# The last 64 keys of two heads as one block-diagonal product, and their flip moved behind the products with v

## The chip, the core and the metric

The kernel runs on one core of one Trainium2 chip. The metric is the device time of one execution in microseconds (us). A core has TensorE (matrix products, PE in the profile; its weight loads stand as PEld), VectorE (DVE), ScalarE (ACT), GpSimd (POOL) and SyncE (SP), which issues most transfers. Each engine works through its own list of instructions in order and waits for others by semaphores.

## The reference, cut to what matters

```python
# q, k, v: (8 batches, 8 heads, 576, 64), f32
scores = q @ k.T / sqrt(64)
scores = where(scores >= max(scores) - tau, scores, -1e9)
attn = exp(scores - max(scores)); attn /= attn.sum() + 1e-9
x = (attn @ v)                       # to (4608, 512)
g = x @ w_gate
out = (g * sigmoid(g) * (x @ w_val)) @ w_out
```

So it is an attention whose scores below a threshold are dropped, and behind it a gated feed-forward block with 512 x 1536 weights.

## The kernel before, in words

Two heads are worked together, as halves of the 128 partitions; four such pairs make a batch. The first batch is treated apart from the other seven, by code that is written out by hand (lines 411 to 755) and whose order of instructions is the order in which Python runs it. From line 758 on, the other batches are placed by a planner (`Plan`), which the change does not touch.

In the first batch a pair's 576 queries are cut into tiles of 128 (t = 0 to 3) and a last one of 64 (t = 4). The list `segs` holds first the "early" tiles t = 0, 1 of all four pairs, eight in all, and then t = 2, 3, 4 of all four pairs, twelve in all. Between the latter TensorE also makes the first products of the feed-forward block (L543). While the first batch runs, the weights are fetched (L277, L280) and taken into another form in pieces: ScalarE reads each piece twice (L296, L297), GpSimd clamps it (L289), VectorE shifts and merges it (L316, L322), GpSimd adds (L324).

A tile goes through these steps:

- `scores` (L417): products of q and k for both heads (L428, for t = 4 L434) into two `sc` tiles; VectorE takes the largest score of each row (L445); ScalarE makes the threshold and the exponential (L448, L449); VectorE drops what lies below the threshold and sums the row (L452), then takes the inverse of the sum, `ri` (L454, L455). For t below `TA` = 2 ScalarE builds per head a diagonal matrix of `ri` (L468), the `unit`; for later tiles the rows are scaled at once (L460 on GpSimd, L462 on ScalarE) and the unit is the identity.
- `flip_steps` (L479): TensorE turns the 128 x 576 values round, by a product with the unit. Per head, four blocks of 128 keys go into a bank `tp` (L496 for the early tiles, L494 later), and the last 64 keys into a bank `end` that both heads share: for the early tiles one 128*64 product per head (L499), behind that head's four blocks; for t = 2, 3 one transposition for both heads (L501); for t = 4 L505. ScalarE copies `tp` (L502) and `end` (L509) out.
- `attend_tile` (L513): the products with v. For the four blocks of 128 keys each head has a 128*64 product into its half of the bank `xa` (L526). The last 64 keys of both heads lie on the two halves of the partitions, and each head has a 64*64 product with its half of `vr2` (L529). ScalarE copies `xa` out (L531).

The loop from L691 runs these for three tiles in turn: it issues the scores of tile n, then the units of tile n - 1 (`next(last)`, L701: L468), then attends tile n - 2 (L702), then flips tile n - 1 (L703 to L709), and so ScalarE's list has L468, L531, L448, L449, L502, L509, L296, L297 in a step. Four banks of PSUM (`bank`, `give_back`, L227) go round among `xa`, `end`, `tp` and the feed-forward products. At the first tile of the second part (n = NP, x = 0) a second `attend_tile` follows in the same step (L711).

`load_v` (L394) fetches v for a pair: the first 512 keys with keys on the partitions (L407), and the last 64 keys of the first head on partitions 0 to 63, of the second head on 64 to 127 (L408), all into the tile `vall`. SyncE issues both.

Of the kernel before, what the change touches and what calls it, by code (L numbers as in the profile page):

```python
# [10 lines left out]
F32 = mybir.dt.float32  # L11
# [101 lines left out]
def kernel(  # L113
# [11 lines left out]
    nc = tc.nc  # L125
    P = 128
    B, H, S, D = q.shape
    NP = H // 2
# [6 lines left out]
    KT = S // P  # L135
    KM = KT * P
    NK = NJ // 2
    SM = 512
    NT = SM // P
# [13 lines left out]
    const = ctx.enter_context(tc.tile_pool(name="const", bufs=1))  # L153
# [22 lines left out]
    WS = NF2 * DM2  # L176
    vall = const.tile([P, 2 * NJ * D], F32, name="vall")
    PB = 24
    pall = const.tile([P, PB * SH], F32, name="pall")
    NQ = 7  # L180
    QW = NF2 // 2 * P
# [45 lines left out]
    def bank(name):  # L227
        n = turns.popleft()
        ps = ps_f.tile([P, 512], F32, name=name, tag=f"bank{n}")
        taken[id(ps)] = n, ps  # L230
        return ps

    def give_back(ps):
        turns.append(taken.pop(id(ps))[0])
# [159 lines left out]
    def load_v(seg):  # L394
        b, hp_ = divmod(seg["i"], NP)
        src = v[b, 2 * hp_:2 * hp_ + 2]
        if seg["halved"]:
            vr = vall[:, 0:NJ * D].rearrange("p (h j d) -> p h j d", h=2, d=D)
            for a in range(2):
                for c in range(2):  # L400
                    nc.sync.dma_start(out=vr[(2 * a + c) * G:(2 * a + c + 1) * G].rearrange("r h j d -> r h (j d)"),
                                      in_=src.rearrange("h (r c j) d -> c r h (j d)", c=2, j=NK)[c])
        else:
            own = vall[:, hp_ * S:(hp_ + 1) * S]
            vr = own[:, 0:2 * KT * D].rearrange("p (h t d) -> p h t d", h=2, d=D), own[:, 2 * KT * D:]
            for h in range(2):
                nc.sync.dma_start(out=vr[0][:, h], in_=src[h, 0:KM].rearrange("(t p) d -> p t d", p=P))  # L407
                nc.sync.dma_start(out=vr[1][h * D:(h + 1) * D], in_=src[h, KM:S])  # L408
        seg["v"] = vr

    heads = [slice(h * D, (h + 1) * D) for h in range(2)]

    def turned(t):
        return TA <= t < NT
# [57 lines left out]
    unflipped, unattended = deque(), deque()  # L472
    xts = {}

    def flip():
        for _ in flip_steps():
            pass

    def flip_steps():  # L479
        if not unflipped:  # L480
            return
        seg, t, both, ps = unflipped.popleft()
        n = P if t < NT else D
        pT = pTbufs[0][:, 0:2 * KT * n].rearrange("p (h t q) -> p h t q", h=2, t=KT)
        pT2 = pTbufs[0][:, 2 * KT * n:(2 * KT + 1) * n]
        pTbufs.rotate(1)
        end = bank("end")
        for h, (p, unit) in enumerate(ps):
            tp = bank("tp")
            for kt in range(KT):  # L490
                at_ = kt * P + (D if turned(t) and h == 1 else 0)
                ks, to = slice(at_, at_ + P), slice(kt * P, (kt + 1) * P)
                if unit is ident:
                    nc.tensor.transpose(tp[:, to], p[:, ks], unit)  # L494
                else:
                    nc.tensor.matmul(tp[:, to], p[:, ks], unit, start=True, stop=True)  # L496
            if t < NT:
                if not turned(t):
                    nc.tensor.matmul(end[h * D:(h + 1) * D, 0:P], p[:, KM:S], unit, start=True, stop=True)  # L499
                elif h == 1:  # L500
                    nc.tensor.transpose(end[:, 0:P], both, unit)  # L501
                nc.scalar.copy(pT[:, h], tp.rearrange("p (t q) -> p t q", q=P))  # L502
            else:
                for hs in heads:
                    nc.tensor.matmul(end[hs, 0:D], p[hs, KM:S], unit[hs, hs], start=True, stop=True)  # L505
                nc.scalar.copy(pT, tp.rearrange("p (t h q) -> p h t q", h=2, q=D))
            give_back(tp)
            yield
        nc.scalar.copy(pT2, end[:, 0:n])  # L509
        give_back(end)  # L510
        unattended.append((seg, t, pT, pT2))

    def attend_tile():  # L513
        if not unattended:
            return
        if not xts:
            for u, lo in enumerate((0, 2 * XW)):
                xts["full", u] = xall[:, lo:lo + XW].rearrange("p (c n) -> p c n", c=NCC)
            xts["last", 0] = xlast
        seg, t, pT, pT2 = unattended.popleft()  # L520
        vr, vr2 = seg["v"]
        n = pT2.shape[1]
        xa = bank("xa")
        for kt in range(KT):
            for h in range(2):
                nc.tensor.matmul(xa[h * D:(h + 1) * D, 0:n], vr[:, h, kt, :], pT[:, h, kt, :],  # L526
                                 start=(kt == 0), stop=False)
        for hs in heads:
            nc.tensor.matmul(xa[hs, 0:n], vr2[hs, :], pT2[hs, :], start=False, stop=True)  # L529
        u, lo = divmod(t * P, TC)  # L530
        nc.scalar.copy(xts[("last", 0) if t == NT else ("full", u)][:, seg["i"], lo:lo + n], xa[:, 0:n])  # L531
        give_back(xa)
# [145 lines left out]
    nc.scalar.activation(junk, minus2, AF.Exp)  # L678
    fetch_weights()
    load_v(segs[0])  # L680
    fetch_weights()
    fetch_qk(2)
    fetch_weights()
    load_v(segs[1])
    fetch_weights()
    fetch_qk(3)
# [4 lines left out]
    for n, seg in enumerate(segs[:2 * NP]):  # L691
# [3 lines left out]
        for x, t in enumerate(seg["tiles"]):  # L695
# [3 lines left out]
            if not n and not x:  # L699
                run_idle(6)  # L700
            next(last, None)  # L701
            attend_tile()  # L702
            flips = flip_steps()  # L703
            if n >= NP and x == 1:
                next(flips, None)
# [4 lines left out]
            if n == NP and x == 0:  # L710
                attend_tile()  # L711
                give(FIRST)
# [23 lines left out]
            if x == 0 and 0 < n < NP - 1:  # L736
                load_v(segs[n + 1])
                more_loads.popleft()()
# [328 lines left out]
    copy_place, s_place = vall[:, 0:NQ * P], whole[:, end_:end_ + DM + P]  # L1067
    e_place = pall[:, PB * SH - DM - P:]
    w_place = pall[:, PB * SH - DM - P - 4 * HW:PB * SH - DM - P].rearrange("p (s n o q) -> p s n o q", s=2, n=4, q=P)
    assert 4 * NQ * P + DM + 4 * HW + DM + P <= PB * SH  # L1070
    s_buf = Buf(s_place[:, 0:DM].rearrange("p (f n) -> p f n", n=TC))
# [859 lines left out]
    own = xall[:, 3 * XW:]  # L1931
    WS = {4: (0, own), 5: (1, ring[:, 1]), 6: (2, own), 7: (3, ring[:, 1]), 8: (4, ring[:, 1]), 9: (5, ring[:, 1])}

    for s, (n, x) in enumerate((n, x) for n in range(len(halved)) for x in range(NU3)):
        seg = halved[n]
        i, t = seg["i"], seg["tiles"][x]
# [4 lines left out]
        if s == 0:  # L1941
            next(last, None)
            attend_tile()
            next(last, None)
            flip()
            plan.t += 2.4
            plan.free.update(DVE=2.0, ACT=2.5)
        elif s == 1:
            attend_tile()
            next(last, None)  # L1950
            plan.t += 1.0
            store_last(0)
# [37 lines left out]
    for c in (B - 1, B):  # L1990
# [4 lines left out]
        if c < B:  # L1995
            w = SM // 2
            j = []
            for kh in range(2):
                src = last_hbm[:, 2 * kh:2 * kh + 2, :].rearrange("p c (t n) -> p t c n", t=2)
# [41 lines left out]
```

## Time and profile before

| what | value |
|---|---|
| median of three runs | 1373.49 us (1373.44 to 1375.5) |
| the profiled execution | 1375.14 us, its span 1373.0 us |
| granted TensorE clock, mean | 0.999 |
| busy share of the span: PE, DVE, ACT, POOL | 99%, 78%, 64%, 53% |
| the chain that ended last: PE's share | 91% |
| scores of the first early tile start | 7.57 us |
| first L468, last L468 | 12.72 us, 53.92 us |
| products of the feed-forward block start (L543) | 58.96 us |
| first scores of the planned batches (L1685) | 134.05 us |

How to read it: a row of a timeline gives the start and the length in us, the engine, the source line, the operation, what it writes and reads, the shape and the number of records; in brackets stands the idle time of the engine ahead of it and what ended that. For TensorE "128*64" is the tile shape: 128 rows (contracted) by 64 columns. An f32 product is recorded twice, a transposition once. TensorE's ends are modelled, so its starts say more than its lengths.

### The profile page before, as it was taken

The page shows a single profiled execution, that of the slowest core. Times are in us where ns is not written, and L with a number is a line of the kernel's source. Part 1 is how long each engine was busy: PE and PEld are TensorE (multiplying, and loading weights), DVE is VectorE, ACT ScalarE, POOL GpSimd, SP SyncE. Part 2 cuts the span into 40 slices and gives each one's busy share as a digit, 9 for nine tenths or more (in the row PEclk, how much of TensorE's full clock was granted, in tenths as well). Part 3 has the DMA queues.
Part 4 walks back from the last instruction along what each step waited for, and adds up shares of the span by engine and source line. Part 5 has one row for each costly group of instructions (what it writes and reads, how often), then busy time and mean ns, then how long its engine had stood idle before and what let it go on. Part 6 is the DMA issues. An engine that isn't in the chain of part 4 may idle for free.

```text
span 1373.0 us, 39266 instructions
## 1 busy us (share of the span) xinstructions
PE 1355.9 (99%) x15630; PEld 1114.8 (81%) x15630; DVE 1071.2 (78%) x2815; ACT 872.6 (64%) x2270; POOL 724.6 (53%) x671
## 2 busy tenths in 40 slices
PE   9999999999999999999999999999999999999998
PEld 6766777778777878878887888878887788999998
DVE  6788888887887777778778777877777776787786
ACT  6888766676766767677677766776767764330330
POOL 2688499744574669534973387437943593000000
PEclk9999999999999999999999999999999999999999
DMA  7752414365524541555154513553165404424421
GB/s 174 196 191 70 102 37 125 107 179 143 174 52 131 147 110 35 170 147 139 37 166 126 155 37 127 139 143 92 30 196 145 112 19 143 161 78 140 154 68 32
DMA packets 208294, 162.32 MB, mean 118 GB/s; under 512 B 166128, under 2 KB 180464, under 8 KB 202736
## 3 DMA queue, kind: packets, MB, share of 16 engines
q1 hardware_dynamic: 203920, 158.86, 41.1%
q8 instruction: 124, 2.03, 0.6%
q10 hardware_dynamic: 4192, 0.95, 0.3%
q14 instruction: 58, 0.48, 0.1%
HBM read 138.28 MB, written 21.50 MB: 116 GB/s over the span
## 4 chain that ended last, share of the span: by engine, by line
PE 91%; ACT 2%; DVE 2%; POOL 1%; DMA 1%; SPq 1%; issue 1%; ACTq 0%; DVEq 0%; POOLq 0%
PE pb L973 18%; PE pa L973 12%; PE px L1453 12%; PE sc L1685 10%; PE xa L1782 9%; PE pe L973 9%; PE po L1249 5%; PE py L1462 5%; PE sc L1134 2%; PE pg L1180 2%; PE pv L1180 2%; PE pe L1134 1%; SPq L357 1%; PE sc L1453 1%; PE xa L526 1%
## 5 line engine op out<-in xcount | busy, mean ns | idle before, releaser
L1733 DVE SCALAR_TENSOR_TENSOR pall<-sc,th,pall 128x288 f32<-128x288 f32 x504 | 243.7, 513 | 64.2 <-ACT pall L1731 49.8
L973 PE MATMUL pb<-xall,big 128*128 128x256 f32 x1152 | 273.5, 380 | 0.0
L1731 ACT ACTIVATE pall<-sc,nm 128x288 f32<-128x288 f32 x504 | 231.9, 497 | 34.1 <-DVE pall L1733 33.5
L973 PEld LDWEIGHTS pb<-xall,big 128*128 128x128 f32 x1152 | 216.4, 190 | 31.0 <-issue 2.5
L1761 DVE STREAM_TRANSPOSE pall<-pall 128x576 f32<-128x576 f32 x252 | 189.5, 764 | 57.0 <-ACT pall L1759 41.8
L1759 ACT ACTIVATE pall<-pall,ri 128x288 f32<-128x288 f32 x408 | 186.2, 526 | 25.7 <-DVE ri L1747 25.2
L973 PE MATMUL pa<-xall,big 128*128 128x256 f32 x768 | 183.3, 382 | 0.0
L827 POOL TENSOR_TENSOR hall<-hall,tmp 128x512 f32<-128x512 f32 x80 | 102.2, 1278 | 152.8 <-DVE hall L1026 136.2
L973 PEld LDWEIGHTS pa<-xall,big 128*128 128x128 f32 x768 | 143.1, 190 | 22.0 <-issue 2.5
L1685 PE MATMUL sc<-kT,qT 64*32 64x144 f32 (+1 forms) x5376 | 150.9, 347 | 2.9 <-DVE pall L1733 2.6
L1706 DVE TENSOR_REDUCE mx<-sc 128x2 f32<-128x576 f32 x168 | 124.6, 742 | 30.2 <-PE sc L1685 29.7
L1685 PEld LDWEIGHTS sc<-kT,qT 64*32 64x32 f32 x5376 | 98.0, 106 | 58.0 <-issue 18.6
L973 PE MATMUL pe<-xall,big 128*128 128x256 f32 x576 | 137.3, 381 | 0.0
L1782 PE MATMUL xa<-pall,vall 64*32 64x288 f32 x4032 | 132.0, 404 | 0.8 <-DVE hall L1026 0.8
L1756 POOL TENSOR_SCALAR pall<-pall,ri 128x288 f32<-128x288 f32 x96 | 95.3, 1004 | 60.5 <-DVE ri L1747 60.4
L973 PEld LDWEIGHTS pe<-xall,big 128*128 128x128 f32 x576 | 108.5, 190 | 17.0 <-issue 2.7
L1782 PEld LDWEIGHTS xa<-pall,vall 64*32 64x32 f32 x4032 | 74.6, 107 | 51.4 <-issue 7.0
L1741 ACT COPY sums<-sums 32x6 f32<-32x6 f32 x336 | 66.6, 198 | 45.1 <-DVE pall L1733 40.5
L827 POOL TENSOR_TENSOR tmp<-tmp 128x512 f32<-128x512 f32 x36 | 45.9, 1275 | 60.2 <-ACT tmp L1048 60.2
L1025 ACT ACTIVATE vall<-tmp 128x512 f32<-128x512 f32 x96 | 60.1, 629 | 25.2 <-POOL tmp L827 9.4
L1462 PE MATMUL py<-wo,hall 128*128 128x256 f32 x336 | 74.8, 379 | 0.0
L1708 DVE TENSOR_REDUCE mx<-sc 128x1 f32<-128x288 f32 x168 | 74.5, 444 | 0.0
(258 smaller groups left out, 2475.5 us busy)
## 6 DMA issues: line engine op xcount, KB each, us to landing
big<-sums_hbm SPq DMA_DIRECT2D x42, 1024.0 KB, 5.3
big<-sums_hbm SPq DMA_DIRECT2D x48, 768.0 KB, 4.9
vall<-in_v_dram SPq DMA_DIRECT2D x112, 144.0 KB, 3.1
out_dram<-big SPq DMA_DIRECT2D x32, 256.0 KB, 3.9
qT<-in_q_dram SPq DMA_DIRECT2D x112, 72.0 KB, 4.6
kT<-in_k_dram SPq DMA_DIRECT2D x112, 72.0 KB, 3.0
wo<-in_moe_w_gate_dram SPq DMA_DIRECT2D x16, 384.0 KB, 4.0
wo<-in_moe_w_val_dram SPq DMA_DIRECT2D x16, 384.0 KB, 4.5
```

The lines of the kernel that those rows point to most:

```text
L827: return lambda: nc.gpsimd.tensor_tensor(out=out, in0=a, in1=b, op=op)
L973: nc.tensor.matmul(ps[:, i], w[:, k_, i * P:(i + 1) * P], x[:, k_, :], start=first and i == k_ == 0, stop=True, skip_group_check=True)
L1453: nc.tensor.matmul(ps, a[:, f, :], ws[n][:, f, :], start=bank_ not in begun, stop=True, skip_group_check=True)
L1462: nc.tensor.matmul(ps(), a[:, f, i * P:(i + 1) * P], operands[o][:, f, :], start=first and f == 0, stop=True, skip_group_check=True)
L1685: nc.tensor.matmul(pss[h][(slice(g * G, (g + 1) * G), *part)], qT[hs, col:col + G], kT[hs, c * SH + keys[0]:c * SH + keys[1]], start=True, ...
L1706: rs.append(job("DVE", 0.72, lambda n=n, tile_=tile_: nc.vector.tensor_reduce(out=mx[:, n:n + 2, 0], in_=tile_[:, :, 0:SH], axis=AX.X, op= ...
L1731: ej = job("ACT", 0.42, lambda x=x, n=n: nc.scalar.activation(ps[x], scs[x], AF.Exp, bias=nm[:, n:n + 1]), ej, *((masks[h, 0], masks[h, 1] ...
L1733: masks[x] = job("DVE", 0.45, lambda x=x, n=n: nc.vector.scalar_tensor_tensor(out=ps[x], in0=scs[x], scalar=th[:, n:n + 1], in1=ps[x], op0 ...
L1756: scaled.append(job("POOL", 1.02, lambda x=x, n=n: nc.gpsimd.tensor_scalar(out=x, in0=x, scalar1=ri[:, n:n + 1], scalar2=None, op0=ALU.mul ...
L1759: scaled.append(job("ACT", 0.46, lambda x=x, n=n: nc.scalar.activation(x, x, AF.Copy, scale=ri[:, n:n + 1]), rj, rank=rank))
L1761: seg["turned"].append(job("DVE", 0.72, lambda both=both: nc.vector.transpose(out=both, in_=both), *scaled, rank=rank))
L1782: nc.tensor.matmul(holds[a].ap()[x * G:(x + 1) * G, 0:SH].rearrange("d (i q) -> d i q", q=G), vr[rs, h, j, ds], p[rs, h, :, j, :], start=( ...
```

## The change

A new tile `vends` has 128 columns for each of the four pairs and is cleared once by GpSimd. `load_v` puts the last 64 keys of the first head into rows 0 to 63, columns 0 to 63 of it, and those of the second head into rows 64 to 127, columns 64 to 127, so that what stands for a pair is a block-diagonal 128 x 128 matrix. In `attend_tile` one 128*128 product with it takes the place of the two 64*64 products, for all twenty tiles of the first batch.

The two L499 of an early tile move. A new function `flip_end` issues them for the tile that is next to be flipped; `attend_tile` calls it between the products of the 128-key blocks and the last product, and `flip_steps` calls it at its start if that has not been done. The values of tile n - 1 are so turned round in the middle of attending tile n - 2, and the bank `end` is kept in the queue `ended` until the flip. Transpositions L501 and L505 stay where they are.

```diff
+    vends = const.tile([P, NP, P], F32, name="vends")
+    nc.gpsimd.memset(vends, 0.0)
...
-            vr = own[:, 0:2 * KT * D].rearrange("p (h t d) -> p h t d", h=2, d=D), own[:, 2 * KT * D:]
+            vr = own[:, 0:2 * KT * D].rearrange("p (h t d) -> p h t d", h=2, d=D), vends[:, hp_]
...
-                nc.sync.dma_start(out=vr[1][h * D:(h + 1) * D], in_=src[h, KM:S])
+                nc.sync.dma_start(out=vr[1][h * D:(h + 1) * D, h * D:(h + 1) * D], in_=src[h, KM:S])
...
+    def flip_end():
+
+        if unflipped and not ended:
+            seg, t, both, ps = unflipped[0]
+            if t < NT and not turned(t):
+                end = bank("end")
+                for h, (p, unit) in enumerate(ps):
+                    nc.tensor.matmul(end[h * D:(h + 1) * D, 0:P], p[:, KM:S], unit, start=True, stop=True)
+                ended.append(end)
...
     def flip_steps():
...
+        flip_end()
         seg, t, both, ps = unflipped.popleft()
...
-        end = bank("end")
+        end = ended.popleft() if ended else bank("end")
...
             if t < NT:
-                if not turned(t):
-                    nc.tensor.matmul(end[h * D:(h + 1) * D, 0:P], p[:, KM:S], unit, start=True, stop=True)
-                elif h == 1:
+                if turned(t) and h == 1:
                     nc.tensor.transpose(end[:, 0:P], both, unit)
...
     def attend_tile():
...
-        for hs in heads:
-            nc.tensor.matmul(xa[hs, 0:n], vr2[hs, :], pT2[hs, :], start=False, stop=True)
+        flip_end()
+        nc.tensor.matmul(xa[:, 0:n], vr2, pT2, start=False, stop=True)
```

More of the change, by code (lines that the diff above doesn't have):

```diff
@@ L473 @@
     xts = {}
+    ended = deque()
+    def flip_end():
[6 more added lines that the diff above has]
+                ended.append(end)
     def flip():
```

## The prediction

> **What bounds the kernel now.** I read the page first. TensorE is busy nearly all the time and its granted clock is full in every slice, so no clock change is in play:
>
> ```profile
> PE 1355.9 (99%) x15630; PEld 1114.8 (81%) x15630; DVE 1071.2 (78%) x2815; ACT 872.6 (64%) x2270; POOL 724.6 (53%) x671
> ```
>
> That line is an average; all touched instructions stand in the first batch, between 12 and 138 us. So next came the chain in order of time (0 to 140 us), the waits of 12 to 58 us, and the timeline of each engine. The chain runs through SyncE's DMA issues up to about 35 us, then through TensorE, ScalarE, VectorE and GpSimd in turn. Within 12 to 58 us the eight early tiles run, one after the other. One step of them (columns: start us, us, engine, line; "x" counts machine records, and a product has two), ScalarE first:
>
> ```profile
> 24.70 0.70 ACT L468 ACTIVATE pall<-pall,ri 128x128 f32<-128x128 f32 x2
> 25.37 0.27 ACT L531 COPY xall<-xa 128x128 f32<-128x128 f32 x1
> 25.54 0.30 ACT L448 ACTIVATE th<-nm,cut 128x1 f32<-128x1 f32 x1
> 25.73 0.73 ACT L449 ACTIVATE pall<-sc,nm 128x576 f32<-128x576 f32 x1
> 26.36 0.29 ACT L448 ACTIVATE th<-nm,cut 128x1 f32<-128x1 f32 x1
> 26.54 0.74 ACT L449 ACTIVATE pall<-sc,nm 128x576 f32<-128x576 f32 x1
> 27.16 0.59 ACT L502 COPY big<-tp 128x512 f32<-128x512 f32 x1
> 27.96 0.59 ACT L502 COPY big<-tp 128x512 f32<-128x512 f32 x1 [0.21 <-PE tp L496]
> 28.44 0.27 ACT L509 COPY big<-end 128x128 f32<-128x128 f32 x1
> 28.60 0.92 ACT L296 ACTIVATE big<-wo 128x768 f32<-128x768 f32 x1
> 29.41 1.02 ACT L297 ACTIVATE big<-wo,minus 128x768 f32<-128x768 uint32 x1
> 30.34 0.68 ACT L468 ACTIVATE pall<-pall,ri 128x128 f32<-128x128 f32 x2
> ```
>
> The reader is to see that ScalarE has one gap in the whole step, 0.21 us at the second L502, and that L531 starts the moment L468 is over. The same step on TensorE:
>
> ```profile
> 24.89 0.43 PE L529 MATMUL xa<-big,vall 64*64 64x128 f32 x4
> 25.26 1.16 PE L496 MATMUL tp<-pall 128*128 128x128 f32 x8
> 26.35 0.43 PE L499 MATMUL end<-pall 128*64 128x128 f32 x2
> 26.71 1.16 PE L496 MATMUL tp<-pall 128*128 128x128 f32 x8
> 27.80 0.43 PE L499 MATMUL end<-pall 128*64 128x128 f32 x2
> 28.16 1.33 PE L428 MATMUL sc<-pall,qT 64*128 64x288 f32 x8
> 29.42 1.09 PE L526 MATMUL xa<-big,vall 128*64 128x128 f32 x16
> 30.44 0.43 PE L529 MATMUL xa<-big,vall 64*64 64x128 f32 x4
> ```
>
> TensorE is full too: start to start 1.26 for L428, 1.02 for L526, 0.37 for L529, 1.09 for each L496 group, 0.36 for each L499, 5.55 us in all. Both engines are the bound at once, and L529 runs while ScalarE is still in L468. That is the point on which the change turns: it moves L499, which needs L468's result, ahead of the last product, whose result L531 fetches, and ScalarE works in program order.
>
> **The change, part by part.** Steps below are those that begin with L468 at 18.86, 24.70, 30.34, 35.91, 42.58, 48.09 and 53.63: seven, each with an attended tile ahead of the flip. (At 12.72 nothing is attended; the two L499 go first, and the scores behind them wait for L452's end at 17.0 as before, so that tile gives nothing.)
>
> *TensorE's work.* A switch of tile shape shows as a gap: the eight records of L496 issue 0.111 us apart ((0.97 - 0.19) / 7 from their weight loads), 0.89 us, but the group takes 1.09, so 0.20 is the switch. Between L529 and the next scores TensorE has now 0.37 + 1.09 + 0.36 + 1.09 + 0.36 = 3.27 us. Changed: the second L499 0.36 and the first at most 0.22 ahead of it, the block-diagonal product two records of 0.111, both L496 groups 1.78, one switch 0.20: 2.56 to 2.78. So TensorE is 0.5 to 0.7 us better off per step.
>
> *ScalarE's wait.* Now L531 starts 0.67 us (0.61 in the next step) behind L468's start. Changed, it stands behind: both L468 (0.71), the signal to TensorE (0.06, from L468 at 42.58 plus 0.39 to L496 at 43.01 it is 0.04), the second L499 with its switch (0.36), the block-diagonal product until its result is there (0.11 + 0.29 = 0.40), the signal back (0.05, as 25.32 to 25.37): 1.58 us. Behind L531 ScalarE needs, from the starts above, 0.17 + 0.19 + 0.63 + 0.18 + 0.62 to the first L502, then 0.48 to the second and 0.48 + 0.16 + 0.81 + 0.93 to the next L468: 4.65 us. The second L502 now comes 0.80 behind the first as it waits for TensorE; changed, TensorE is ahead of it, and 0.48 is enough (at 38.82 two took 0.94 to the next start). Changed step: 1.58 + 4.65 = 6.23 us, against 5.57 from 30.34 to 35.91: **+0.66 us**. What queues behind the waiting L531 is L448 and L449, so L452 on VectorE, so the next scores. TensorE does not become the bound: the scores' second head waits for L452's end, 4.4 us into the step; L526 follows 1.29 later (40.27 to 41.56) and its last record 0.77 after that, at 6.46, before L468's first result at 6.23 + 0.43 = 6.66.
>
> *Absorbed.* The delay takes the place of older waits in one step, that from 35.91:
>
> ```profile
> 37.19 0.29 ACT L448 ACTIVATE th<-nm,cut 128x1 f32<-128x1 f32 x1 [0.42 <-DVE nm L445]
> ...
> 40.81 0.90 ACT L296 ACTIVATE big<-wo 128x768 f32<-128x768 f32 x1 [0.76 <-DMA wo<-in_moe_w_val_dram]
> ```
>
> The second waits for a transfer that was issued at 36.79 in SyncE's own row of transfers, with nothing of ScalarE ahead of it: it lands at the same time, and ScalarE comes late enough. Carried step by step (L468 after, against before): 25.09 (+0.39; the first step already has L531 at 0.96), 31.32 (+0.98), 37.55 (+1.64), 43.76 (+1.18, both waits gone), 50.09 (+2.00, with 0.1 for VectorE, which has L661 as well there), 56.32 (+2.69). In the last step the second L502 starts 1.58 + 2.27 behind that, at 60.17 instead of 56.94: **+3.2 us**, and the L526 that waits for it at 57.58 carries this on.
>
> *Later tiles.* Behind 58 us there are 13 more L529, each of which falls from 0.37 to 0.22, as no switch stands between it and the 128*128 work that follows: at most 13 x 0.15 = 1.95 us, at least 0. On the chain TensorE is the limit right behind L529 at 58.6 and 130.4; elsewhere the chain goes from L526 to ScalarE, where only the end of the result counts (0.43 now, 0.40 then), or through GpSimd's L460 with TensorE waiting 1.1 us. I take 2 x 0.15 and 0.1: **-0.4 us**. All starts behind 58 us hang on earlier work of the program, so the rest moves as it is.
>
> *The Trainium skill against it.* In this trace the pair L529 holds its slot for 0.37 us including one switch. "TensorE: Matmul & The Clock Gate", section Why this matters for your kernels, says that small products in separate row and column groups run at the same time, which speaks against the change: the pair already costs the array no more than one product. By that rule the array's part of the late gain is nothing, and if the switch cost nothing either, the sum would be +3.2. "TensorEngine Tiling (Array Packing)", Key Properties, says that changing the tiling mode drains the engine, which is the 0.2 us of the rows.
>
> *The rest.* GpSimd clears 128x512 once: 128x1 took 0.10 us and 128x128 0.20, so some 0.5 us (bounds 0.2 and 2) at 0.7 us, where its next need is 10.49 and the first transfer into the tile is issued at 8.46. It costs nothing below 7 us. The transfers of v keep number, size and place in the queue. The bank order of the flips stays: a rotation is written out the same way, and each bank that L499 takes was emptied a step earlier.
>
> Sum: 3.2 - 0.4 = **+2.8 us**. The profiled execution took 1375.14 us (span 1373.0 and 2.14 around it), 1.65 above the median of the runs shown; there it is 1377.9, on the median 1373.49 + 2.8 = **1376.3**.
>
> **Rivals.** (1) *TensorE is what counts*: the saved switches come through, 7 x 0.5 to 0.7 in the steps and up to 1.9 later: 3.5 to 6.8 us less, 1369. For it: TensorE has no gap in a step. Against: ScalarE has only 0.2 us to give. It decides if L531 starts less than about 0.93 us behind L468 (0.64 now plus the 0.29 regained at L502). 0.13. (2) *The wait is mostly covered*, by waits for transfers in more steps than one, or by TensorE arriving late at L526 anyway: half the early loss and a late gain near 1: +0.6, 1374.1. 0.12. (3) *Nothing is absorbed*, because the transfer at 40.81 moves along and VectorE adds slips in the steps with key transposes: 7 x 0.66 + 0.4: +5, 1378.5. 0.08. (4) The forecast, 0.67; its own ends: a step between +0.5 and +0.8, and a late gain of 0 to 1.9, give +0.9 to +4.1, so 1374.4 to 1377.6.
>
> **The numbers.** The range takes in the forecast's ends, rival 2, and the near part of rival 3, and leaves out rival 1: 1372.5 to 1378.5. A measurement of this kernel can tell about 0.2%, 2.75 us, from no change; the forecast stands on that line, so its 0.67 is split nearly in half (0.30 same, 0.37 slower, as slips rather add). Same: 0.30 + 0.12 = 0.42; slower: 0.37 + 0.08 = 0.45; faster: 0.13.
>
> **What would show it.** In the profile after: L531's copy waits about 0.85 us for the block-diagonal product in the early steps; L468 repeats every 6.2 us; the second L502 waits no more; L468 of the last step stands near 56.3; the steps behind 58 us are as long as before. If L468 repeats every 5 us, rival 1 holds. The forecast is wrong if TensorE's signal and switch take clearly more or less than 0.36 + 0.40, or if the step from 35.91 does not give back its 1.2 us.

## The result and the profile after

The changed kernel took 1381.53 us (median of 5 runs, 1378.44 to 1382.28) against 1375.50 us of the kernel before beside it (5 runs, 1373.44 to 1376.26): a ratio of 1.0039, 95% interval 1.0025 to 1.0054. On a second chip it was 1382.13 against 1376.08, 1.0039 [1.0026, 1.0052] (run a_again below). By the ratio it is slower by 5.4 us [3.4, 7.4], where 2.8 was forecast, and the time lies above the range. The profiled execution of it took 1378.44 us, its span 1376.3. Every line number behind 180 is larger in it: L468 is L470, L531 is L544, L448 and L449 are L450 and L451, L502 is L515, L509 is L522, L296 and L297 are L298 and L299; L496 is L511, L499 is L486, L529 is L542, L526 is L539, L452 is L454, L1685 is L1698.

(A slip in the kernel's description above: the units, L468, are issued by the fourth `next(go)` at L724, at the end of the step before, not by `next(last)` at L701. The order of ScalarE's list is as told.)

The page's engine line of the changed kernel (busy us, share of the span, records):

```profile
PE 1354.6 (98%) x15590; PEld 1117.3 (81%) x15590; DVE 1074.0 (78%) x2815; ACT 872.1 (63%) x2270; POOL 724.9 (53%) x672
```

TensorE has 40 products and 40 weight loads fewer, twenty f32 products at two records each, and is yet later at the end. The timeline of ScalarE in the changed kernel, one early step (start, length, engine, line; in brackets the idle time ahead and what ended it):

```profile
31.41 0.73 ACT L470 ACTIVATE pall<-pall,ri 128x128 f32<-128x128 f32 x2
33.08 0.27 ACT L544 COPY xall<-xa 128x128 f32<-128x128 f32 x1 [0.94 <-PE xa L542]
33.24 0.30 ACT L450 ACTIVATE th<-nm,cut 128x1 f32<-128x1 f32 x1
...
34.87 1.08 ACT L515 COPY big<-tp 128x512 f32<-128x512 f32 x2
35.81 0.30 ACT L522 COPY big<-end 128x128 f32<-128x128 f32 x1
35.97 0.96 ACT L298 ACTIVATE big<-wo 128x768 f32<-128x768 f32 x1
36.77 1.06 ACT L299 ACTIVATE extra<-wo,minus 128x768 f32<-128x768 uint32 x1
37.68 0.72 ACT L470 ACTIVATE pall<-pall,ri 128x128 f32<-128x128 f32 x2
```

And TensorE in the same step:

```profile
30.86 1.09 PE L539 MATMUL xa<-big,vall 128*64 128x128 f32 x16
31.91 0.72 PE L486 MATMUL end<-pall 128*64 128x128 f32 x4
32.55 0.49 PE L542 MATMUL xa<-big,vends 128*128 128x128 f32 x2
32.88 1.95 PE L511 MATMUL tp<-pall 128*128 128x128 f32 x16
35.17 2.02 PE L430 MATMUL sc<-pall,qT 64*128 64x288 f32 x8 [0.35 <-DVE pall L454]
```

The gap of 0.21 us at the second L502 is gone, and one of 0.94 stands at L544, which comes 1.67 us behind the units instead of 0.67. The step is 6.27 us; TensorE, which had no gap, now has one. The units start at 12.72, 18.88, 25.14, 31.41, 37.68, 44.43, 50.67 and 56.94 us (before 12.72, 18.86, 24.70, 30.34, 35.91, 42.58, 48.09, 53.63). The first products of the feed-forward block start at 62.87 (+3.9 us) and the first planned scores at 137.98 (+3.9).

Behind 140 us two further things differ. The first is the clock. The page's row of the granted clock for the kernel before shows only nines:

```profile
PEclk9999999999999999999999999999999999999999
```

But a nine means 0.9 or more, and a slice is 34 us long. The table by stretches, on the kernel before (stretch and its length; busy time and records of PE, PEld, DVE, ACT and POOL; granted clock, DMA share, GB/s), has a hole that a slice can't show:

```profile
147.90:151.30 3.40, 3.40 (x74) 2.46 (x58) 3.37 (x8) 0.59 (x3) 2.45 (x2) 0.50 0.07 23
```

There the 64 scores took 3.08 us against 1.72 at 134.05. The changed kernel's profile has no such stretch, which hides some 1.4 us of its loss: its lag on TensorE is 4.0 us at these scores (150.91 against 146.86) and 2.5 behind them (153.87 against 151.34). The second is a row of small stalls. The scores of a planned tile, 32 f32 products in one burst and so 64 records, on the kernel before and then on the changed kernel:

```profile
347.75 1.70 PE L1685 MATMUL sc<-kT,qT 64*32 64x288 f32 x64
```

```profile
350.42 1.41 PE L1698 MATMUL sc<-kT,qT 64*32 64x288 f32 x41
352.44 0.69 PE L1698 MATMUL sc<-kT,qT 64*32 64x144 f32 x23 [0.61 <-issue]
```

The burst breaks off behind its 41st record, and the profile names nothing that it waits for ("issue"). The same happens at 648 us behind the 35th (0.35 us). TensorE's idle time behind 155 us is 3.03 us, before 1.97.

### The profile page after: what moved, and what is told of

The parts are those of the page before. It is cut to its first block, busy times and chain, and to the rows that moved or that the text cites. A ratio compares the mean times of both kernels' runs of the same rounds, so it can differ in the third digit from the quotient of the medians.

```text
span 1376.3 us, 39173 instructions
## 1 busy us (share of the span) xinstructions
PE 1354.6 (98%) x15590; PEld 1117.3 (81%) x15590; DVE 1074.0 (78%) x2815; ACT 872.1 (63%) x2270; POOL 724.9 (53%) x672
## 4 chain that ended last, share of the span: by engine, by line
PE 90%; ACT 2%; DVE 2%; SPq 2%; POOL 1%; DMA 1%; issue 1%; ACTq 0%; DVEq 0%; POOLq 0%
PE pb L986 18%; PE pa L986 12%; PE px L1466 12%; PE sc L1698 10%; PE xa L1795 9%; PE pe L986 9%; PE po L1262 5%; PE py L1475 5%; PE sc L1147 2%; PE pg L1193 2%; PE pv L1193 2%; SPq L359 1%; PE pe L1147 1%; PE sc L1466 1%; PE pv L556 1%
## 5 line engine op out<-in xcount | busy, mean ns | idle before, releaser
L1698 PE MATMUL sc<-kT,qT 64*32 64x144 f32 (+1 forms) x5376 | 149.7, 346 | 4.2 <-DVE pall L1746 3.0
L1698 PEld LDWEIGHTS sc<-kT,qT 64*32 64x32 f32 x5376 | 97.7, 106 | 58.6 <-issue 19.2
```

The lines of the kernel that those rows point to most:

```text
L1698: nc.tensor.matmul(pss[h][(slice(g * G, (g + 1) * G), *part)], qT[hs, col:col + G], kT[hs, c * SH + keys[0]:c * SH + keys[1]], start=True, ...
```

## The experiments

Three sets, each on one chip with runs of the kernel before among them: 1376.32 us there (35 runs) in the first, 1376.08 (30) in the second, 1375.73 (29) in the third. "First planned" is the start of the first planned scores in the profiled execution (before 134.05).

**The theory**: L544 waits in ScalarE's order, as the forecast has it, and this makes the early steps longer. The rivals: the block-diagonal product, or the cleared tile, costs the time; or it is lost behind the first batch, where the change does nothing.

### e1_diag: the block-diagonal product alone

```diff
(the kernel before, with vends, its two transfers, and)
-        for hs in heads:
-            nc.tensor.matmul(xa[hs, 0:n], vr2[hs, :], pT2[hs, :], start=False, stop=True)
+        nc.tensor.matmul(xa[:, 0:n], vr2, pT2, start=False, stop=True)
```

> The block-diagonal product alone; the two L499 stay behind the four blocks of their head. Theory (the place of L499 costs, as ScalarE's copy of xa then stands behind L468, L499 and the product): no new wait, an early step stays at 5.5 to 5.6 us, the planned batches' first scores start at 133.5 to 134.1 us (134.05 before, 137.98 in the changed kernel), the time is within 1 us of the kernel before. Rival (the product with the cleared tile, its full 128x128 weight load or its place in memory costs): at least half of the loss is here, first scores at 136 us or later, ratio 1.002 or more.

Measured: 1379.59 us, 1.0022 [1.0012, 1.0031]. Steps 5.55 to 5.69 us apart from the first and the two from 36.98 and 44.12 (7.14, 6.11); the copy 0.80 to 0.96 behind the units. First planned 136.25, but 1.2 us of this lag stands already at 13.9 us, behind a stretch of half clock from 7.6 to 11.0. So most early steps are not longer, and yet the kernel is slower. By the time and the first planned scores the rival's signs are there; that the product is not the reason is shown below, by e3_pad22, which has it and loses nothing, and by b_pad42f, which loses as much without it.

### e2_flip: the earlier flip alone

```diff
(the changed kernel)
-        nc.tensor.matmul(xa[:, 0:n], vr2, pT2, start=False, stop=True)
+        for hs in heads:
+            nc.tensor.matmul(xa[hs, 0:n], vr2[hs, :], pT2[hs, :], start=False, stop=True)
```

> The early flip of the last keys alone, with the two 64*64 products behind it. Theory: the whole wait is here and one more switch of tile shape stands in it, so an early step takes 6.3 to 6.5 us, the first planned scores start at 138 to 139.5 us, ratio 1.003 to 1.006. Rival (the block-diagonal product costs): step 5.6, first scores near 134, ratio 1.000.

Measured: 1379.01 us, 1.0020 [1.0011, 1.0028]. Steps 6.19 to 6.32, first planned 137.52. ScalarE's row has the wait of the changed kernel, without its new product:

```profile
26.81 0.27 ACT L543 COPY xall<-xa 128x128 f32<-128x128 f32 x1 [0.90 <-PE xa L541]
```

So the wait in the early steps is the moved flip's alone. The whole loss is smaller than expected (1.003 to 1.006).

### e3_behind: both parts, the two L486 behind the last product

```diff
-        flip_end()
         nc.tensor.matmul(xa[:, 0:n], vr2, pT2, start=False, stop=True)
+        flip_end()
```

> Both parts, but the two L499 stand behind the block-diagonal product instead of ahead of it. Theory: the copy of xa waits for nothing that ScalarE has yet to make; it starts 0.6 us behind L468 again, a step takes 5.4 to 5.6 us, first planned scores at 133 to 134 us, the time is that of the kernel before or up to 1 us less. Rival (the work itself, not its order, costs): a step of 6.2 us and 138 us as in the changed kernel.

Measured: 1378.13 us, 1.0019 [1.0004, 1.0033]. Two instructions change places, and the step is as before the change, 5.61 us:

```profile
24.69 0.70 ACT L470 ACTIVATE pall<-pall,ri 128x128 f32<-128x128 f32 x2
25.54 0.27 ACT L544 COPY xall<-xa 128x128 f32<-128x128 f32 x1 [0.15 <-PE xa L541]
...
30.30 0.70 ACT L470 ACTIVATE pall<-pall,ri 128x128 f32<-128x128 f32 x2
```

The feed-forward products start at 58.45, 0.5 us ahead of the kernel before. The early wait is gone, and the kernel is still slower by 2.6 us. (First planned was 135.80 and not 133 to 134, behind a half clock from 122.1 to 128.9 us.) The theory holds for the steps and fails for the time: something else costs as much.

### e4_copylate: the copy of xa behind the two exponentials

```diff
+        if late:
+            copies.append(copy)
+        else:
+            copy()
...
+            while copies:
+                copies.popleft()()
```

> The changed kernel with one move on ScalarE: in the steps of the early tiles the copy of xa stands behind the two exponentials instead of ahead of them. Nothing on TensorE moves. Theory (the loss is ScalarE's program order): the exponentials no longer wait, TensorE's blocks come 0.65 us later than in the kernel before, so a step takes 5.8 to 6.0 us, first planned scores at 135 to 136.5 us, ratio about 1.001 to 1.002. Rival (TensorE itself is late, or the product costs): no change against the changed kernel, 138 us.

Measured: 1378.58 us, 1.0018 [1.0010, 1.0027]. The copy waits no more, since ScalarE does the exponentials meanwhile; now the second L515 waits 0.31 us for TensorE, and the step is 5.80 to 5.85 (7.10 once). First planned 135.72.

What e1, e3 and e4 share with the changed kernel is not a wait of the first batch but a shorter list of TensorE: 79, 87 and 88 instructions fewer in the trace, e2 only 12. Their bursts at 350 us break too, and the place moves with the count: behind the 36th record in e1, the 40th in e3 and the 41st in e4. The page tells how the list reaches the engines. Its rows of the queues on the kernel before (packets, MB, share):

```profile
q8 instruction: 124, 2.03, 0.6%
...
q14 instruction: 58, 0.48, 0.1%
```

2.51 MB for 39,266 instructions are 64 bytes each, and a packet of q8 holds 16.4 KB, that is 256 of them; 124 such packets are 31,744 of the 31,783 instructions of TensorE. The stalls at 352 and 648 us stand 2.3 to 2.4 us behind the start of such a packet. That gave the **second theory**: what is left of the loss comes from where the fetches cut TensorE's list. It can be tested with instructions that do nothing: a tiny f32 product (32*32, 8 columns) is four, two records of the product and two weight loads.

```python
def run_tiny(n):
    ps = bank("idle")
    for i in range(n):
        g = slice(i % 4 * G, (i % 4 + 1) * G)
        nc.tensor.matmul(ps[g, 0:8], ones[g, 0:G], ones[g, 0:8], start=True, stop=True)
    give_back(ps)
```

Each edit below is one call of it behind the first `run_idle(6)`, where TensorE idles 1.83 us (b_pad42 has a second one elsewhere); 22 of them took 0.55.

### a_again: the changed kernel beside the next three

> The changed kernel as it is, beside the others on one chip. Early-wait theory: steps of 6.25 to 6.28 us, first planned scores at 138.0 (134.05 before). If that shift of 3.9 us is all, the ratio to the kernel before is 1.0028; if TensorE's stalls behind 155 us (3.01 us idle in its first profile, 1.94 before) belong to this program rather than to one execution, they stand again at about 352 and 648 us, and the ratio is some 1.0030 to 1.0040.

Measured: 1382.13 us, 1.0039 [1.0026, 1.0052]. Its profile, another execution on another chip, has the first stall at the same record, the second too (behind the 35th, 0.34 us):

```profile
355.01 1.41 PE L1698 MATMUL sc<-kT,qT 64*32 64x288 f32 x41
357.04 0.69 PE L1698 MATMUL sc<-kT,qT 64*32 64x144 f32 x23 [0.62 <-issue]
```

So these two places belong to the program, not to the moment. A third stall, 0.32 us at 909.65, is in this profile alone.

### a_pad22: the changed kernel with 22 tiny products

```diff
     run_idle(6)
+    run_tiny(22)
```

> The changed kernel with 22 tiny products (32*32, 8 columns) in TensorE's first idle time, 88 instructions, which give TensorE's later instructions the places in its list that they have before the change. Theory that the stalls at 352 and 648 us come from where the fetches of instructions fall: both vanish, idle time of TensorE behind 155 us near 1.9 instead of 3.0 us, the time 0.5 to 1.5 us under that of the changed kernel, first planned scores still at 138. Rival, that the stalls come from the time shift itself or by chance: same places, same time as the changed kernel within 0.5 us.

Measured: 1379.02 us, 1.0020 [1.0009, 1.0031]: 3.1 us less than the changed kernel beside it, for 22 products more. Early steps 6.27 to 6.32, first planned 137.76, so the early loss is all there; but the burst is whole, and the lag on the kernel before, 3.7 us at the first planned scores, is 3.5 at the end:

```profile
351.27 1.70 PE L1706 MATMUL sc<-kT,qT 64*32 64x288 f32 x64
```

Its list is not free of stalls. One stands in another burst, behind the 39th record:

```profile
499.67 1.40 PE L1706 MATMUL sc<-kT,qT 64*32 64x288 f32 x39
501.55 0.70 PE L1706 MATMUL sc<-kT,qT 64*32 64x144 f32 x25 [0.47 <-issue]
```

### b_pad42: the kernel before with 42, of them 27 in place of an idle run

```diff
     run_idle(6)
+    run_tiny(21)
...
-                run_idle(6)
+                run_tiny(27)
```

> The kernel before with 42 more tiny products in idle time of TensorE (168 instructions, which shifts its list by as much, modulo 256, as the change does). Theory that the places of the fetches make the stalls: steps and first planned scores as before (134.05), but stalls of some 0.6 and 0.35 us at about 350 and 645 us, idle time of TensorE behind 155 us near 3 us, and 0.5 to 1.5 us more time. Rival, that the stalls follow the time shift or chance: no stalls at these places, time as before within 0.5 us.

Measured: 1379.41 us, 1.0027 [1.0016, 1.0037], with stalls, but inconclusive: the 27 tiny products left TensorE idle for 2.19 us where the six large ones left no gap, the clock was halved from 12.8 to 19.7 us, and first planned was at 137.63.

### b_pad42f and b_pad64: the kernel before with 42 and with 64, all in the first idle time

```diff
     run_idle(6)
+    run_tiny(42)
```

> The kernel before with 42 tiny products in TensorE's first idle time, where they should take 1.1 of 1.83 us; nothing else moves. 168 instructions shift the rest of TensorE's list as the change does, counted modulo the 256 that one fetch of 16 KB brings (88 fewer there). Theory of the places of the fetches: first planned scores at 134.05, stalls of about 0.6 at 348 and 0.35 at 644 us as in the changed kernel, idle time of TensorE behind 155 us near 3 us, time 1 to 3 us over the kernel before. Rival, that the stalls follow from the change's time shift: as the kernel before within 0.5 us.

> The same with 64 tiny products, 256 instructions, one whole fetch. Theory of the places of the fetches: no stalls at 348 and 644 us, time as the kernel before within 0.7 us (the products take 1.6 of 1.83 us). Rival, that tiny products as such cost later time: at least as slow as with 42 of them.

Measured: 42 give 1379.08 us, 1.0024 [1.0011, 1.0036]; 64 give 1375.57 us, 0.9997 [0.9987, 1.0007]. This is the test that decides: the kernel before, with no part of the change. 168 instructions more are the place modulo 256 of 88 fewer, and the burst breaks behind the same 41st record as in the changed kernel; 256 more are the old place, and it is whole. First with 42, then with 64:

```profile
348.93 1.41 PE L1693 MATMUL sc<-kT,qT 64*32 64x288 f32 x41
350.69 0.69 PE L1693 MATMUL sc<-kT,qT 64*32 64x144 f32 x23 [0.34 <-issue]
```

```profile
348.42 1.70 PE L1693 MATMUL sc<-kT,qT 64*32 64x288 f32 x64
```

First planned stood 1.9 (64) and 2.4 us (42) late in the profiles, not at 134.05. With 64 the step from 35.91 took 7.80, as VectorE's shift of a weight piece took 2.16 us beside an addition of GpSimd's (told below under what is absorbed); with 42 the step from 42.56 took 7.98, under a half clock from 42.9 to 46.3. So one profile of the early steps is not a measurement of them, and the timed runs decide: more tiny products are not slower as such.

The traces show the place itself. If TensorE's records (products, weight loads and waits) are counted from the first in the order of their starts, every stall marked "issue" behind 155 us (24 of 0.16 to 1.18 us, in all traces but that of the kernel before) stands at place 193 or 194 of a block of 256. The programs with the old places cross the same edges in other bursts: a_pad22, e3_pad22, e6_pad22 and b_pad64 all stall behind the 39th record of the burst at 495 to 500 us (0.16 to 0.52 us), and the kernel before has two bursts that are too long there, without a gap in the rows, where 1.70 is usual:

```profile
496.16 1.98 PE L1685 MATMUL sc<-kT,qT 64*32 64x288 f32 x64
```

```profile
937.16 2.36 PE L1685 MATMUL sc<-kT,qT 64*32 64x288 f32 x64
```

So the number of instructions does not make the stalls; it decides which bursts they cut.

### e3_pad22: neither the wait nor the shifted list

```diff
(e3_behind)
     run_idle(6)
+    run_tiny(22)
```

> Both parts of the change, the two last-key products behind the block-diagonal one, and 22 tiny products in the first idle time, so that neither ScalarE's early wait nor the places of the fetches differ from the kernel before. If these two are all that the change costs: steps of 5.5 to 5.7 us, first planned scores at 133 to 134.5, no stalls at 350 and 647 us, and a time 0 to 1.5 us under the kernel before. If a third cost stands behind 155 us: 1 us or more over it.

Measured: 1376.54 us, 1.0002 [0.9991, 1.0014]. No stalls at 350 and 647 us, one of 0.48 at 500. Both costs removed, the change is worth nothing that can be measured; the gain of up to 1.5 us did not come. (In its profile two early steps took 7.4 and 7.6 us, for the same two reasons as above, and first planned was 137.32.)

### e6_pad22: an order that suits ScalarE

```diff
(e3_behind with the late copy and the 22 tiny products, and in early steps)
+            first = t < TA
+            if first:
+                next(go)
+                next(go)
             if n or x:
                 split_weights()
```

> The block-diagonal product with the two last-key products behind it, the copy of xa behind the two exponentials, the units ahead of the two reads of the weight piece in early steps, and the same 22 tiny products. Theory that ScalarE's order and its waits set the early steps: steps of 5.3 to 5.5 us, products of the feed-forward block at 57 to 58.4 (58.96 before), first planned scores at 132.5 to 134, and with the list's places restored a time 0 to 1.5 us under the kernel before. Rival, that the weight transfers or VectorE set the steps: steps stay at 5.6 to 5.7 or one of them takes the gain back, first planned at 134 to 136.

Measured: 1374.51 us, 0.9992 [0.9979, 1.0005]. The units stand ahead of the two reads of the weight piece, and the steps fall to 5.39 to 5.48, but the one from 33.74 took 7.20 and gave it back: VectorE's largest score came 1.21 us late there. First planned 134.13. It is faster than the changed kernel by far and can't be told from the kernel before, although its profile has two stalls (0.52 us at 497, 0.95 at 754).

## Why the prediction was wrong

Ordered by the two causes, the ratios nearly add up:

| | TensorE's list at its old places (0 or 1 off, modulo 256) | list shifted (79 to 88 fewer, or 168 more) |
|---|---|---|
| no early wait | e3_pad22 1.0002, b_pad64 0.9997 | e1 1.0022, e3 1.0019, b_pad42f 1.0024 |
| early wait | a_pad22 1.0020 | the change 1.0039 |

Two runs stand outside. e2 has the early wait and a list shifted by 12, with three stalls of 2.0 us together in its profile, and yet only 1.0020; its runs had the highest mean clock, 0.9995, and the seven at 1.000 took 1378.9 us on average, 4.0 more than the kernel before at that clock. e4 has seven steps longer by some 0.25 us (0.0013) and the shifted list (0.0019), which would make about 1.003, and measured 1.0018 [1.0010, 1.0027]. So a sum of the two is good to about 1 us.

**ScalarE's wait** was right. The copy came 1.64 to 1.68 us behind the units (forecast 1.58), the step 6.24 to 6.27 apart from one (6.23), the wait 0.94 (0.85), the second L502 waits no more, and rival 1 is out: TensorE's saving only gave it a gap. Some 0.05 us per step make 0.3 in all.

**What is absorbed** was right in place and not in size. The transfer's wait of 0.76 us went: L298 at 42.72 waits for nothing. But VectorE's wait of 0.42 did not go in each execution; the step from 37.68 was to take 6.21 us, and took 6.75. The rows of GpSimd, VectorE and ScalarE of the changed kernel show what stood there:

```profile
35.66 1.82 POOL L326 TENSOR_TENSOR big<-big 128x768 uint32<-128x768 uint32 x1
```

```profile
36.15 1.75 DVE L318 TENSOR_SCALAR big<-big 128x768 uint32<-128x768 uint32 x1
...
39.24 1.38 DVE L447 TENSOR_REDUCE nm<-sc 128x1 f32<-128x576 f32 x2
```

```profile
39.98 0.30 ACT L450 ACTIVATE th<-nm,cut 128x1 f32<-128x1 f32 x1 [0.37 <-DVE nm L447]
```

L318 takes 0.54 us alone (at 43.26). Here it ends at 37.90, 0.42 behind the end of GpSimd's L326 at 37.48. The same pair in a_pad22 ends at 36.93 and 37.34 (L318 1.05 us long, no wait behind it, step 6.29) and in a_again at 38.08 and 38.49 (2.21 us, a wait of 0.83, step 7.20). In b_pad64 and e3_pad22 (2.16 and 2.17 us) it is 0.42 again. In all five VectorE's instruction ends 0.41 to 0.42 us behind GpSimd's, however long it has been "running": it reads as if it began only then, and where GpSimd's add falls decides over 0.9 us of the step. The Trainium skill, "SBUF — State Buffer", section Who interferes with whom, has the rule: VectorE and GpSimd share one pair of ports; where an instruction of VectorE in a mode with two ports meets one of GpSimd, the one that issues first holds the pair to its end and the other blocks; it names tensor_scalar among those that can enter such a mode. The five pairs of rows agree; that the ports are the cause was not tried apart. The forecast moved VectorE's rows as they were and did not ask what would stand beside them.

**The late gain** of 0.4 us was not there. The product's slot is 0.33 us (32.55 to 32.88), not 0.22; it was 0.37. The skill's rule that the prediction weighed against its own row came closer: two small products in separate groups had already cost hardly more than one. From the first products of the feed-forward block to the first planned scores the lag stayed at 3.9 us.

**"The rest moves as it is"** failed. The forecast argued that behind 58 us all hangs on earlier work of the program. It counted what each instruction costs and not that fewer of them move every later one to another place of TensorE's list, modulo 256: +3.1 us by a_again and a_pad22, +3.3 by b_pad42f, with nothing of the change in it. This is the step that failed: the forecast gave it nothing. The Trainium skill, "Runtime: NRT & Kernel Launch", section Instruction fetch mechanics, has 256 instructions in a block of 16 KiB and calls the crossing mostly hidden. The rows agree with the size, and mostly is not always: of the 124 blocks of TensorE's list one to three show as a stall in each of these traces, always at the same place of the block.

**"No clock change is in play"** failed too: it was read from a row of nines. Among the runs of the kernel before in the three sets, those with a mean granted clock of 1.000 took 1374.8 us on average (28 runs), with 0.999 1376.2 (42), with 0.998 1377.0 (18). Much of the scatter goes with it. The forecast stood on a median of three, 1373.49, where the later ones are 1375.5 to 1376.3; that the clock made this difference is not shown, as those three runs have no clock on record. Of the 5.2 us between forecast and result 2.0 are this base and 3.1 the shifted list. The early part, by a_pad22 +2.8 us [1.2, 4.3], is as large as the whole forecast, in part by luck: the forecast had 3.2 early and 0.4 gained late, and the profiles had 3.9 at the first planned scores and no late gain.

**Open** is why the shifted list costs 3 us. The starts of the planned scores, from the fifth burst (181.02 us in the kernel before) to the end, show part of it: there the lag on the kernel before grew by 1.9 us in a_again and by 0.0 in a_pad22, by 1.3 with 42 tiny products and by -0.5 with 64, but by 0.6 only in the first profile of the changed kernel. So some 1.8 us of each pair's difference stand behind 181 us. The clock may be the rest: over the timed runs its mean was lower by 0.001 (a_again 0.9979, a_pad22 0.9988; 42 0.9982, 64 0.9993), which by the figures above is some 1.1 us. But the first five runs of the changed kernel, at 0.9992, lost as much, and that the stalls lower the clock is not shown. Why some edges of the blocks stall and most do not was not tried either.

## What to carry to other kernels

An instruction moved ahead of another on a busy engine delays everybody who waits for the latter, and an engine that works in order passes the delay on: price the wait on the consumer's list, not the time saved on the producer's. A change that alters the number of instructions has a second effect, at the edges of the blocks of 256 in which they are fetched, which here was as large as the first; try the kernel with a few empty instructions in an idle stretch before a difference of 0.2% is put down to the edit. And when two engines can block each other, look at what will run side by side after the shift, not only at how long each took.

## What the runs showed of the hardware that was not expected

- TensorE's clock was halved for stretches of 3.4 or 6.8 us, at varying places: 147.9 us in the profile of before, none in the first of the change, in e2_flip or in b_pad64, 7.6 and 151.0 in e1_diag, 122.1 and 149.4 in e3_behind, 42.9 in b_pad42f. Several lie close to the idle time in front of the second planned scores (1.75 us in the kernel before), but not all.
- The edge of a block of 256 of TensorE's instructions can show as "issue" in the middle of a burst of small products: 24 times in twelve traces, 0.16 to 1.18 us, at place 193 or 194 of the block each time, and at the same record in three executions of two different kernels.
- An instruction of VectorE whose length grows from 0.54 to 1.05, 1.75 or 2.2 us need not work more slowly: all of them ended 0.41 to 0.42 us behind the end of one of GpSimd's.
